# Reads of weight sums moved behind those of the second MLP's inputs, and gates and first scans moved ahead, in a one-core linear-attention and two-MLP kernel

## The chip, the cores and the metric

The kernel runs on one core of one Trainium2 chip. The metric is the device time of one execution in microseconds. Beside the timed runs there is one execution taken by the hardware profiler; all rows below are from it. Engines are named as in the profile: PE is TensorE (PEld its weight load), ACT is ScalarE, DVE is VectorE, POOL is GpSimd, SP is SyncE, which issues nearly all DMAs from one in-order queue.

## What is computed

A gated linear attention (4 batches, 8 heads, 768 positions, head size 48), then a gated MLP with an RMS norm (384 to 1536 to 384), then a second MLP with a squared ReLU (384 to 2048 to 384), all in fp32:

```
f = 1 / (1 + exp(-f_logit))
for t in range(S):
    state = f[:, :, t, :, None] * state + einsum('bhd,bhe->bhde', k[:, :, t], v[:, :, t])
    y[:, :, t] = einsum('bhd,bhde->bhe', q[:, :, t], state)
x = y as (3072, 384)
xn = x / sqrt(mean(x * x) + 1e-6) * rms_g
x = (silu(xn @ w_gate) * (xn @ w_val)) @ w_out
out = (relu(x @ w_in) ** 2) @ w_out2
```

## The kernel before

**Work and stages.** The attention is cut into 24 units: a chunk of 128 positions of one batch (six chunks, four batches). Four units fill a group of 512 tokens, and the first MLP runs over six groups. To keep fp32 accuracy every matmul of the MLPs is made three times, with operands split into a high and a low part (`fp32r`); ACT makes the high part, DVE subtracts it for the low part.

The opening `first()` follows an order written by hand: it converts the first MLP's weights, computes units 0 to 7 and runs group 0. `phase1()` runs groups 1 to 5. A group has 12 steps f; each has three *blocks* of nine 512-column matmuls on PE: G (gate projection), V (value projection) and O (output projection, of the step before). I write G5 for block G of step 5. After G, ACT computes the sigmoid product `sg`; after V, DVE multiplies it with V (L971, "the product"), ACT rounds it to `hh` (L974), and DVE makes `hl` (L976). G and V have one PSUM bank each: block G of a step needs the sigmoid of the step before to be done, block V the product of the step before. `phase2()` runs the second MLP over four sets of 768 tokens; its weight products use 15 sums of weights and inputs instead of 18 products.

**What sets the order.** Between the blocks `phase1` puts other work by *segments*: three a step, numbered through, segment s of group gi beginning at 36 gi. `plan_unit(u, s)` gives each instruction of an attention unit a segment relative to s, that of its scores: `load_gates` at -9 (DMA of both gates' logits), `gate` at -3 (two ACT passes over 128x1024: L296, L297), `scan_b` at -2 (DVE scan of the reversed gates and a reciprocal: L308, L309) with `keep_end` (ACT), `scan_a` and `mul_k` at -1 (second DVE scan, product with k: L316, L319), `mul_q` (L322) and `scores` at 0, `kv` at 6, `state_add` (DVE, L492) at 7. In a segment the planned work stands ahead of the first MLP's own sigmoid, product or rounding. Scores use two PSUM banks; one of them also holds `kv` of the unit before until `state_add` has read it. Units 8 to 23 are planned so; 8 to 11 stand closer together (scores at segments 40, 47, 54, 60) than the later ones (nine segments apart).

`plan_work` places the conversion of the second MLP's weights: loads of the raw 64-bit words, bit operations (L561, L568, L578), sums of weight blocks (`w2_sum`, L710), splits (`w2_split`: ACT L664, DVE L665) and their writes to DRAM (L667). It goes through these jobs in order and gives each the first segment at which a count of planned DVE and ACT time stays under a cap. `gate` and `scan_b` are part of that count, so moving them moves conversion jobs.

**The end of the first MLP.** In group 5 (`last0` is its first segment) the job `open` closes the pools of the raw words and the attention (`open_late`) and at once starts eight reads of weight sums, `wa` (L1031, 384 KB each), into the pool opened in their place. From segment `last0 + 9` the job `x3` reads the second MLP's inputs `x3` (L1051: three tiles, each in a piece of 512 and one of 256 columns) into slots that weights of the first MLP have left. From segment `last0 + 12` the jobs `("x", p)` split them and their sums into `xc` (ACT L1092, DVE L1093; sums L1081). The first split (p = 9) reads tile `x3_0`, the second a difference of `x3_0` and `x3_2`, the third a sum with `x3_1`. SP waits for a DMA's slot, and for the DMA eight issues earlier, before it issues; what stands behind waits too.

Of the kernel before, what the change touches and what calls it, by code (L numbers as in the profile page):

```python
# [22 lines left out]
KT = DM // P  # L23
# [166 lines left out]
def tile_linear_attention_moe(  # L190
# [29 lines left out]
    N = UG * C  # L220
    NT = 3 * C
# [449 lines left out]
    def w2_plain(key, nm, a, b):  # L671
        if nm not in w2t:
            w2t[nm] = w2_tile(nm)
        w2_split(key, w2f[key], w2t[nm][:, a], w2t[nm][:, b])
# [37 lines left out]
    def w2_part(i, c):  # L712
        t, b = w2c[i, c]
        w2_split(("c", i, c), t[:, b], t[:, 2 + b], t[:, b])

    def w2_spare(i, key):
        t, _ = w2c[i, 2]
        w2_split(key, w2f[key], t[:, 1], t[:, 3])
# [34 lines left out]
    def at(where, s, fn):  # L753
        where.setdefault(max(s, NG), []).append(fn)
# [3 lines left out]
    def plan_unit(u, s):  # L758
        starts[u] = s
        for k, fns in (  # L760
            (-9, (load_gates,)), (max(-9, starts.get(u - 2, 0) + 7 - s), (load_v,)),
            (max(-9, starts.get(u - 2, 0) + 9 - s), (load_qk,)),
            (-3, (gate,)), (-2, (scan_b, keep_end)), (-1, (scan_a, mul_k)),
            (0, (mul_q, k_turn, decay)), (1, (masked,)), (2, (k_back,)), (3, (norm, power)), (4, (x_scale,)),
            (5, (x_turn, kcopy)), (6, (x_back,)), (7, (state_add,)), (10, (x_high, x_low)),
        ):
            for fn in fns:
                if fn not in (load_gates, load_qk, load_v) or u > 2 * UG:
                    at(side, s + k, lambda fn=fn: fn(u))
                    planned.setdefault(s + k, []).append(fn.__name__)  # L770
        for k, fn in ((0, scores), (2, attend), (6, kv)):
            at(tail, s + k, lambda fn=fn: fn(u))
            room[s + k] = room.get(s + k, 0) + TAIL[fn.__name__]

    NG = 3 * F1
    for gi in range(1, NU - 1):
# [3 lines left out]
        scan_b=(1.4, 0), keep_end=(0, 0.2), scan_a=(1.2, 0), mul_k=(0.7, 0), mul_q=(0.7, 0), masked=(1.4, 0),  # L780
# [23 lines left out]
    def job(name, fn, dve=0.0, act=0.0, after=()):  # L804
        work.append((name, fn, (dve, act), after))

    def conversion(pair, after=()):
        job(("load", pair), lambda: w2_load(pair), after=after)

    def bits(pair, after=()):  # L810
        job(("scale", pair), lambda: w2_scale(pair), act=0.9, after=((("load", pair), 3),) + after)
        for n, c in enumerate((0.55, 0.96, 0.96)):
            job(("bits", pair, n), lambda n=n: w2_bits(pair, n), dve=c, after=((("scale", pair), 1),))

    def sums(i, cs, after=()):
        for n, x in enumerate(W_SUMS[cs]):
            act = x[1] == "="
            job(("sum", i, cs, n), lambda n=n: w2_sum(i, cs, n), dve=0 if act else 0.3, act=0.3 if act else 0, after=after)

    def split(name, fn, after=()):  # L820
        job(name, fn, dve=0.56, act=0.51, after=after)

    def plan_work():
        gone = ()
        for i in range(F2 // 3):
            a = tuple(("a", 3 * i + f) for f in range(3))
            b = tuple(("b", 3 * i + f) for f in range(3))
            pa, pb, pc = (a[0], a[1]), (a[2], b[0]), (b[1], b[2])
            if i == 0:
                conversion(pa)  # L830
                conversion(pb)
            bits(pa)
            bits(pb)
            sums(i, (0, 1))
            for c in (0, 1):
                split(("part", i, c), lambda i=i, c=c: w2_part(i, c), ((("sum", i, (0, 1), 5), 1),))
            sums(i, (2,))
            split(("part", i, 2), lambda i=i: w2_part(i, 2), ((("sum", i, (2,), 3), 1),))
            split(("plain", b[0]), lambda i=i, k=b[0]: w2_spare(i, k))
            sums(i, (3, 4), after=((("part", i, 1), 2),))  # L840
            conversion(pc, after=((("plain", b[0]), 2),))
            for c in (3, 4):
                split(("part", i, c), lambda i=i, c=c: w2_part(i, c), ((("sum", i, (3, 4), 5), 1),))
            bits(pc)
            if i + 1 < F2 // 3:
                na, nb = (("a", 3 * i + 3), ("a", 3 * i + 4)), (("a", 3 * i + 5), ("b", 3 * i + 3))
            else:
                na, nb = (("a", F2 - 1), ("b", F2 - 1)), None
            for n, k in enumerate(pc):
                split(("plain", k), lambda k=k, n=n, nm=f"b{3 * i + 1}": w2_plain(k, nm, 2 * n, 2 * n + 1))  # L850
                if n == 0:
                    conversion(na, after=((("bits", pc, 2), 1),))
            if nb:
                conversion(nb, after=((("plain", pc[1]), 2),))
        bits(na)
        for n, k in enumerate(na):
            split(("plain", k), lambda k=k, n=n: w2_plain(k, "last", 2 * n, 2 * n + 1))
        job(("open",), open_late, after=((("plain", na[1]), 1), (None, last0 + 2)))
        job(("x3",), lambda: (x3_tiles(), x3_load(0)), after=((None, last0 + 9),))
        freed = [2, 6, 8, 12, 14, 18, 20, 24, 26, 30, 32, 36]  # L860
        for n, p in enumerate(X_KEYS):
            f = next(f for f, c in enumerate(freed) if c >= n + 4)
            at_least = ((None, last0 + 3 * (f + 1) + 3), (("x3",), 3))
            for q in X_NEEDS.get(p, ()):
                job(("xsum", q), lambda q=q: x_sum(q, r_tile(f"xs_{q}")), dve=0.56, after=at_least)
            split(("x", p), lambda p=p: (x_tile(p), x_split(p)))
            work[-1] = work[-1][:3] + (at_least,)

        for b in range(10):
            f = next(f for f, c in enumerate(freed) if c >= b + 21)  # L870
            job(("b", b), lambda b=b: fetch_b(b), after=((None, last0 + 3 * (f + 1) + 3),))

        for name, fn, cost, after in work:
            s = max([NG, when.get("last", 0)] + [when[a] + g if a else g for a, g in after])
            while any(c and (busy(s)[e] + c > CAP + room.get(s, 0) or crowd(s, e) + c > 0) for e, c in enumerate(cost)):
                s += 1
            for e, c in enumerate(cost):
                busy(s)[e] += c
            when[name] = when["last"] = s
            at(side, s, fn)  # L880
# [7 lines left out]
    pend, nxt, parts = [], [], []  # L888
# [124 lines left out]
    def open_late():  # L1013
        upper.close()
        L["as"] = pool("late_w", bufs=8, reuse_waits="tile")
        L["r"] = pool("late_r", bufs=18, reuse_waits="tile")
        for c in range(8):
            fetch_part()

    parts_order = [(s, i, c) for s in range(NS) for i in range(NSET + 1) for c in ((0, 1, 4, 2, 3) if i < NSET else (0,))]  # L1020
    part_tiles = {}
# [2 lines left out]
    def fetch_part():  # L1024
        if fetched[0] == len(parts_order):
            return
        s, i, c = parts_order[fetched[0]]
        fetched[0] += 1
        t = L["as"].tile([P, 2, DM], F32R, tag="as", name=f"wa{s}_{i}_{c}")
        src = w2d["c", i, c] if i < NSET else w2d["a", F2 - 1]  # L1030
        nc.sync.dma_start(t.bitcast(F32), src)  # L1031
        part_tiles[s, i, c] = t
# [6 lines left out]
    def r_tile(nm):  # L1039
        return L["r"].tile([P, NT], F32, tag="r", name=nm)  # L1040

    def x3_tiles():
        L["x3"] = [wp.tile([P, 2, NT], F32, tag="w", name=f"x3_{k}") for k in range(KT)]

    def x3_load(s):
        o, g = 2 * NT * s, 0
        while g < 2 * NT:
            gi, c = divmod(o + g, N)
            n = min(N - c, 2 * NT - g)
            for k in range(KT):  # L1050
                nc.sync.dma_start(  # L1051
                    L["x3"][k].rearrange("p a t -> p (a t)")[:, g:g + n], x3d[gi][:, k, c:c + n]
                )
            g += n

    def xb(k, j):
        return L["x3"][k][:, j]
# [6 lines left out]
    def x_tile(p):  # L1064
        XT[p] = wp.tile([P, 2, NT], F32R, tag="w", name=f"xc{p}")
# [9 lines left out]
    def x_sum(p, t):  # L1075
        def arg(x):
            return xb(*x) if isinstance(x, tuple) else XS[x]

        XS[p] = t
        op, a, b = X_SUMS[p]  # L1080
        nc.vector.tensor_tensor(t, arg(a), arg(b), op=ALU.add if op == "+" else ALU.subtract)  # L1081
# [7 lines left out]
    def x_split(p, put=None):  # L1089
        src = xb(*X_PLAIN[p]) if p in X_PLAIN else XS[p]  # L1090
        t = XT[p]
        nc.scalar.copy(t[:, 0], src)  # L1092
        (put or run)(lambda: nc.vector.tensor_sub(t[:, 1], src, t[:, 0].bitcast(F32)))  # L1093
# [335 lines left out]
```

## Time and profile before

| | |
|---|---|
| median of 3 runs | 957.01 us (955.17 to 957.71) |
| profiled execution | 951.61 us |
| its span in the trace | 949.7 us |
| PE busy | 923.9 us (97%) |
| DVE, ACT busy | 644.6 us (68%), 488.5 us (51%) |
| mean granted PE clock | 0.988 of full speed |

The span is the time between the first and the last instruction of the trace; the execution's own time is 1.9 us more. A row of a wait list names who waited and for whom; a row of a timeline gives start, duration, and in brackets the idle time before it with what ended it. An idle engine costs nothing by itself: only what delays the end of PE's work does. The granted clock is given as a share of full speed: 1.00 is 2.4 GHz, 0.50 is 1.2 GHz.

### The profile page before, as it was taken

The page shows a single profiled execution, that of the slowest core. Times are in us where ns is not written, and L with a number is a line of the kernel's source. Part 1 is how long each engine was busy: PE and PEld are TensorE (multiplying, and loading weights), DVE is VectorE, ACT ScalarE, POOL GpSimd, SP SyncE. Part 2 cuts the span into 40 slices and gives each one's busy share as a digit, 9 for nine tenths or more (in the row PEclk, how much of TensorE's full clock was granted, in tenths as well). Part 3 has the DMA queues.
Part 4 walks back from the last instruction along what each step waited for, and adds up shares of the span by engine and source line. Part 5 has one row for each costly group of instructions (what it writes and reads, how often), then busy time and mean ns, then how long its engine had stood idle before and what let it go on. Part 6 is the DMA issues. An engine that isn't in the chain of part 4 may idle for free.

```text
span 949.7 us, 15747 instructions
## 1 busy us (share of the span) xinstructions
PE 923.9 (97%) x5945; PEld 813.3 (86%) x5945; DVE 644.6 (68%) x1147; ACT 488.5 (51%) x1020; POOL 31.4 (3%) x54
## 2 busy tenths in 40 slices
PE   6899999989999999999998899999999999999997
PEld 4778877878888888788887689999999999999997
DVE  7899967666777777766643635756775677666552
ACT  6876654544455544454441425556555554655451
POOL 3210000000000000000000000000000000000000
PEclk8899999999999999999999899999999999999999
DMA  9456434466457467455256056540744075406300
GB/s 340 178 190 215 154 136 121 144 203 199 124 192 219 132 207 242 146 201 172 70 180 232 1 199 240 193 151 24 232 148 151 4 240 167 125 17 190 118 26 29
DMA packets 78387, 148.48 MB, mean 156 GB/s; under 512 B 17248, under 2 KB 44000, under 8 KB 78304
## 3 DMA queue, kind: packets, MB, share of 16 engines
q1 hardware_dynamic: 78304, 147.39, 47.4%
q8 instruction: 49, 0.80, 0.4%
q14 instruction: 34, 0.28, 0.1%
HBM read 115.12 MB, written 32.24 MB: 155 GB/s over the span
## 4 chain that ended last, share of the span: by engine, by line
PE 89%; DVE 3%; DMA 2%; ACT 1%; issue 0%; SPq 0%; ACTq 0%; DVEq 0%
PE o L730 7%; PE o L728 7%; PE o L729 7%; PE X L1105 7%; PE Y L1105 6%; PE v L728 5%; PE g L728 5%; PE acc L728 5%; PE v L730 5%; PE v L729 5%; PE acc L730 5%; PE acc L729 5%; PE g L730 5%; PE g L729 5%; PE sc L341 2%; PE T L1105 2%
## 5 line engine op out<-in xcount | busy, mean ns | idle before, releaser
L730 PE MATMUL o<-wb,h 128*128 128x384 f32 x384 | 128.6, 335 | 0.0
L729 PE MATMUL o<-wb,h 128*128 128x384 f32 x384 | 128.3, 334 | 0.0
L728 PE MATMUL o<-wb,h 128*128 128x384 f32 x384 | 128.3, 334 | 0.0
L974 ACT CAST hh<-sg 128x512 fp32r<-128x512 f32 x72 | 44.7, 621 | 112.3 <-DVE sg L971 112.2
L971 DVE TENSOR_TENSOR sg<-v,sg 128x512 f32<-128x512 f32 x72 | 49.5, 688 | 54.4 <-PE v L730 52.3
L1105 PE MATMUL X<-xc,wa 128*128 128x384 f32 x360 | 82.5, 336 | 0.0
L730 PEld LDWEIGHTS o<-wb,h 128*128 128x128 f32 x384 | 72.1, 188 | 0.5
L728 PEld LDWEIGHTS o<-wb,h 128*128 128x128 f32 x384 | 72.1, 188 | 0.0
L729 PEld LDWEIGHTS o<-wb,h 128*128 128x128 f32 x384 | 72.1, 188 | 0.0
L966 ACT ACTIVATE sg<-g 128x512 f32<-128x512 f32 x72 | 42.7, 594 | 55.8 <-PE g L730 52.9
L1105 PE MATMUL Y<-xc,wa 128*128 128x384 f32 x300 | 68.3, 335 | 0.0
L1105 PEld LDWEIGHTS X<-xc,wa 128*128 128x128 f32 x360 | 63.7, 188 | 1.8 <-ACT d L1180 1.2
L1184 DVE TENSOR_TENSOR c<-T,c 128x384 f32<-128x384 f32 x40 | 22.3, 557 | 52.5 <-PE T L1105 43.4
L976 DVE TENSOR_TENSOR hl<-sg,hh 128x512 fp32r<-128x512 f32 x72 | 49.3, 685 | 7.8 <-ACT hh L974 7.8
L1105 PEld LDWEIGHTS Y<-xc,wa 128*128 128x128 f32 x300 | 53.3, 188 | 0.7 <-DVE c L1184 0.6
L1135 DVE TENSOR_TENSOR h<-d,h 128x384 fp32r<-128x384 f32 x60 | 32.8, 554 | 26.2 <-ACT h L1134 26.1
L728 PE MATMUL g<-xh,wh_o 128*128 128x512 f32 x108 | 43.8, 406 | 4.8 <-ACT sg L966 4.8
L1134 ACT CAST h<-d 128x384 fp32r<-128x384 f32 x60 | 30.2, 511 | 34.4 <-PE o L730 34.4
L1180 ACT COPY d<-X 128x384 f32<-128x384 f32 x40 | 19.1, 478 | 54.7 <-PE X L1105 54.7
L728 PE MATMUL v<-xh,wh_v 128*128 128x512 f32 x108 | 43.8, 406 | 0.2 <-DVE sg L971 0.2
L728 PE MATMUL v<-xh,wh_g 128*128 128x512 f32 x108 | 43.9, 406 | 0.0
L728 PE MATMUL g<-xh,wh_g 128*128 128x512 f32 x108 | 43.6, 404 | 0.0
(192 smaller groups left out, 2240.9 us busy)
## 6 DMA issues: line engine op xcount, KB each, us to landing
wa<-w2d_c SPq DMA_DIRECT2D x100, 384.0 KB, 3.4
raw<-in_w_dram SPq DMA_DIRECT2D x18, 768.0 KB, 4.3
ff<-in_ff_dram SPq DMA_DIRECT2D x20, 516.0 KB, 4.5
qk<-in_qk_dram SPq DMA_DIRECT2D x20, 512.0 KB, 6.2
w2d_c<-ws_c SPq DMA_DIRECT2D x50, 192.0 KB, 4.2
raw_a<-in_w_dram SPq DMA_DIRECT2D x22, 384.0 KB, 4.4
wb<-w2d_b SPq DMA_DIRECT2D x16, 384.0 KB, 3.7
v<-in_vp_dram SPq DMA_DIRECT2D x24, 192.0 KB, 4.6
```

What stands on the lines that cost most here:

```text
L728: nc.tensor.matmul(o, lh, rh, start=first, stop=False)
L729: nc.tensor.matmul(o, lh, rl, start=False, stop=False)
L730: nc.tensor.matmul(o, ll, rh, start=False, stop=last)
L966: nc.scalar.activation(dd["s", f], dd["g", f], AF.Silu)
L971: nc.vector.tensor_mul(dd["s", f], dd["v", f], dd["s", f])
L974: nc.scalar.copy(dd["h", f][0], dd["s", f])
L976: nc.vector.tensor_sub(dd["h", f][1], dd["s", f], dd["h", f][0].bitcast(F32))
L1105: nc.tensor.matmul(o, w[a], x[:, b], start=first and n == 0, stop=last and n == 2, skip_group_check=True,)
L1134: nc.scalar.copy(t[:, 0], r)
L1135: later(lambda: nc.vector.tensor_sub(t[:, 1], r, t[:, 0].bitcast(F32)))
L1180: nc.scalar.copy(t, bk[b])
L1184: nc.vector.tensor_add(t, bk[b], t)
```

## The change

Three edits. `gate` goes from segment -3 to -5 and `scan_b` with `keep_end` from -2 to -3. The eight first reads of weight sums leave `open_late` and become a job `parts`, two segments or more after the job `x3`. And `x3_load` reads tile by tile, in the order 0, 2, 1, both pieces of a tile together, where it had read the first pieces of all tiles and then the second ones.

```diff
@@ plan_unit
-            (-3, (gate,)), (-2, (scan_b, keep_end)), (-1, (scan_a, mul_k)),
+            (-5, (gate,)), (-3, (scan_b, keep_end)), (-1, (scan_a, mul_k)),
@@ plan_work
         job(("x3",), lambda: (x3_tiles(), x3_load(0)), after=((None, last0 + 9),))
+        job(("parts",), lambda: [fetch_part() for _ in range(8)], after=((("x3",), 2),))
@@ open_late
         L["r"] = pool("late_r", bufs=18, reuse_waits="tile")
-        for c in range(8):
-            fetch_part()
@@ x3_load
-        o, g = 2 * NT * s, 0
-        while g < 2 * NT:
-            gi, c = divmod(o + g, N)
-            n = min(N - c, 2 * NT - g)
-            for k in range(KT):
+        for k in (0, 2, 1):
+            o, g = 2 * NT * s, 0
+            while g < 2 * NT:
+                gi, c = divmod(o + g, N)
+                n = min(N - c, 2 * NT - g)
                 nc.sync.dma_start(
                     L["x3"][k].rearrange("p a t -> p (a t)")[:, g:g + n], x3d[gi][:, k, c:c + n]
                 )
-            g += n
+                g += n
```

On SP, in group 5, behind the last write of a plain weight (`w2d_b_15`), the kernel before has the reads `wa` (of eight alike, the first and the last stand here) and then those of `x3`:

```order
L667 DMA w2d_b_15_5256<-ws_last_5250 128x384 x2
L1031 DMA wa0_0_0_5281<-w2d_c_0_0_1884 128x768
...
L1031 DMA wa0_1_4_5295<-w2d_c_1_4_3092 128x768
L1051 DMA x3_0_5321<-x3d_0_81 128x512
L1051 DMA x3_1_5322<-x3d_0_81 128x512
L1051 DMA x3_2_5323<-x3d_0_81 128x512
L1051 DMA x3_0_5321<-x3d_1_82 128x256
```

The same place of the changed kernel:

```order
L667 DMA w2d_b_15_5256<-ws_last_5250 128x384 x2
L1050 DMA x3_0_5305<-x3d_0_81 128x512
L1050 DMA x3_0_5305<-x3d_1_82 128x256
L1050 DMA x3_2_5307<-x3d_0_81 128x512
L1050 DMA x3_2_5307<-x3d_1_82 128x256
L1050 DMA x3_1_5306<-x3d_0_81 128x512
L1050 DMA x3_1_5306<-x3d_1_82 128x256
L1030 DMA wa0_0_0_5339<-w2d_c_0_0_1886 128x768
```

The six reads of `x3` now stand directly behind the writes and ahead of all eight `wa`, and the first two fill tile 0.

On ACT, at the beginning of group 1 (`x3o` is the copy of group 0's result, `ff8` the gates of unit 8, `sg_1_0` and `hh_1_0` the sigmoid and the rounding of step 0), before:

```order
L909 COPY x3o_0_2_1517<-acc_0_2_719 128x512
L966 ACTIVATE sg_1_0_1537<-g_1_0_1521 128x512
L296 ACTIVATE ff8_1430<-ff8_1430 128x8x128
L297 ACTIVATE ff8_1430<-ff8_1430,half_92 128x8x128
L974 CAST hh_1_0_1552<-sg_1_0_1537 128x512
L312 COPY ends_94<-ff8_1430 128x4
```

and now:

```order
L910 COPY x3o_0_2_1517<-acc_0_2_719 128x512
L296 ACTIVATE ff8_1430<-ff8_1430 128x8x128
L297 ACTIVATE ff8_1430<-ff8_1430,half_92 128x8x128
L967 ACTIVATE sg_1_0_1539<-g_1_0_1521 128x512
L312 COPY ends_94<-ff8_1430 128x4
L975 CAST hh_1_0_1555<-sg_1_0_1539 128x512
```

Unit 8's gate has moved ahead of the sigmoid (it can't go further, since segment 36 is the first), and the copy of the ends ahead of the rounding. From unit 10 on the gate stands between a sigmoid and its rounding.

On DVE, in step 7 of group 1, between the first scan of unit 11 and the state addition of unit 10 (`ws_c0_2`, `ws_c0_3` hold weight sums, `qk11` k and q of unit 11), before:

```order
L308 SCALAR_TENSOR_TENSOR ff11_1904<-ff11_1904,floor_89 128x516
L309 RECIPROCAL seed_90<-ff11_1904 128x4
L971 TENSOR_TENSOR sg_1_7_2079<-v_1_7_2081,sg_1_7_2079 128x512
...
L665 TENSOR_TENSOR ws_c0_2_1983<-ws_c0_2_1983 128x384
L665 TENSOR_TENSOR ws_c0_2_1983<-m_a2_1647,ws_c0_2_1983 128x384
L710 TENSOR_TENSOR ws_c0_3_2152<-m_a2_1647 128x128
L710 TENSOR_TENSOR ws_c0_3_2152<-ws_c0_3_2152,m_a2_1647 128x128
L710 TENSOR_TENSOR ws_c0_3_2152<-m_a0_1577,ws_c0_3_2152 128x128
L492 TENSOR_TENSOR state2_99<-kv10_2158,state2_99 48x4x48 x2
```

and now:

```order
L308 SCALAR_TENSOR_TENSOR ff11_1907<-ff11_1907,floor_89 128x516
L309 RECIPROCAL seed_90<-ff11_1907 128x4
L404 SCALAR_TENSOR_TENSOR xg10_2094<-y10_2036,rs10_2075,gB_96 128x384
L665 TENSOR_TENSOR ws_c0_2_1931<-ws_c0_2_1931 128x384
L972 TENSOR_TENSOR sg_1_7_2082<-v_1_7_2084,sg_1_7_2082 128x512
...
L665 TENSOR_TENSOR ws_c0_2_1931<-m_a2_1710,ws_c0_2_1931 128x384
L710 TENSOR_TENSOR ws_c0_3_2152<-m_a2_1710 128x128
L710 TENSOR_TENSOR ws_c0_3_2152<-ws_c0_3_2152,m_a2_1710 128x128
L710 TENSOR_TENSOR ws_c0_3_2152<-m_a0_1577,ws_c0_3_2152 128x128 x2
L710 TENSOR_TENSOR ws_c0_3_2152<-m_a0_1577 128x128
L492 TENSOR_TENSOR state2_99<-kv10_2161,state2_99 48x4x48 x2
```

Between the product of step 7 and the state addition there is one split subtraction (L665) less and there are two sums (L710) more; the scan stands ahead of the product in both. PE's instructions and their order are the same in both kernels.

## Rows read from the trace of the kernel before

**Rows 1.** The page: busy time, share of the span and instructions of each engine.

```profile
PE 923.9 (97%) x5945; PEld 813.3 (86%) x5945; DVE 644.6 (68%) x1147; ACT 488.5 (51%) x1020; POOL 31.4 (3%) x54
```

**Rows 2.** PE's waits, whole span: waiter and releaser, us in total, times, longest.

```profile
PE g L728 <- ACT sg L966: 4.8, 1, 4.8
...
PE sc L341 <- DVE state L492: 2.6, 1, 2.6
...
PE sc L341 <- DVE qk L322: 1.2, 1, 1.2
```

**Rows 3.** Timeline of PE, group 5: start, us, engine, line, operation, [idle before].

```profile
513.53 0.39 PE L728 MATMUL g<-xh,wh_g 128*128 128x512 f32 x1
...
519.43 0.39 PE L730 MATMUL acc<-hh,wl_v 128*128 128x512 f32 x1
524.57 0.79 PE L728 MATMUL g<-xh,wh_o 128*128 128x512 f32 x1 [4.76 <-ACT sg L966]
...
542.28 0.50 PE L728 MATMUL v<-xh,wh_v 128*128 128x512 f32 x1 [0.23 <-DVE sg L971]
```

**Rows 4.** Stretches: us; busy us of PE, PEld, DVE, ACT, POOL; PEclk; DMA; GB/s.

```profile
195.00:200.00 5.00, 2.91 (x22) 2.52 (x23) 3.15 (x8) 0.00 (x0) 0.00 (x0) 1.00 0.92 246
...
525.00:526.00 1.00, 1.00 (x3) 0.73 (x3) 0.64 (x2) 0.29 (x1) 0.00 (x0) 0.50 0.00 0
```

**Rows 5.** Timeline of ACT, group 5, steps 3 and 4.

```profile
512.49 0.62 ACT L974 CAST hh<-sg 128x512 fp32r<-128x512 f32 x1 [2.18 <-DVE sg L971]
521.91 0.51 ACT L1092 CAST xc<-x 128x384 fp32r<-128x384 f32 x1 [8.80 <-DMA x<-x3d]
...
523.93 0.59 ACT L966 ACTIVATE sg<-g 128x512 f32<-128x512 f32 x1
```

**Rows 6.** Timeline of SP's DMA issues, group 5: start, us of all in the row.

```profile
505.13 0.89 SPq L667 DMA_DIRECT2D w2d_b<-ws_last  x2
507.79 5.13 SPq L1031 DMA_DIRECT2D wa<-w2d_c  x8
513.02 4.79 SPq L1051 DMA_DIRECT2D x<-x3d  x6
```

**Rows 7.** DMA issues of the whole span: count, KB each, median us to landing.

```profile
ff<-in_ff_dram SPq DMA_DIRECT2D x20, 516.0 KB, 4.5
...
x3d<-x3o SPq DMA_DIRECT2D x18, 256.0 KB, 2.3
...
x<-x3d SPq DMA_DIRECT2D x12, 256.0 KB, 4.8
```

**Rows 8.** Timelines of ACT and DVE, group 1, unit 8.

```profile
130.61 1.96 ACT L909 COPY x3o<-acc 128x512 f32<-128x512 f32 x3 [2.01 <-PE acc L730]
...
134.57 1.05 ACT L296 ACTIVATE ff<-ff 128x1024 f32<-128x1024 f32 x1
...
136.85 0.62 ACT L974 CAST hh<-sg 128x512 fp32r<-128x512 f32 x1
...
138.21 0.67 DVE L976 TENSOR_TENSOR hl<-sg,hh 128x512 fp32r<-128x512 f32 x1
...
140.51 0.68 DVE L322 TENSOR_TENSOR qk<-qk,ff 128x512 f32<-128x512 f32 x1
```

**Rows 9.** Timeline of DVE, group 1, ahead of unit 11's scores.

```profile
189.74 0.68 DVE L971 TENSOR_TENSOR sg<-v,sg 128x512 f32<-128x512 f32 x1
...
194.91 0.55 DVE L665 TENSOR_TENSOR ws_c<-m_a,ws_c 128x384 fp32r<-128x384 f32 x1
195.38 0.28 DVE L710 TENSOR_TENSOR ws_c<-m_a 128x128 f32<-128x128 f32 x1
...
196.23 0.72 DVE L492 TENSOR_TENSOR state<-kv,state 48x192 f32<-48x192 f32 x2
```

**Rows 10.** Timelines of SP and ACT, group 2, gates of unit 14.

```profile
242.80 0.43 SPq L284 DMA_DIRECT2D ff<-in_ff_dram  x1
...
251.26 0.60 ACT L966 ACTIVATE sg<-g 128x512 f32<-128x512 f32 x1 [1.29 <-PE g L730]
...
254.09 0.62 ACT L974 CAST hh<-sg 128x512 fp32r<-128x512 f32 x1 [2.23 <-DVE sg L971]
```

## Prediction

> **What bounds the kernel now.** First the busy line of the page: TensorE is busy for 97% of the span and VectorE, the next engine, for 68% (PEld is TensorE's own weight load) [rows 1]. So time can only be won where TensorE waits or runs slowly, and I read TensorE's waits next. After the opening part (the first 50 us, which the change leaves alone) only three are above 0.3 us: 4.8 us for a sigmoid of the first MLP, 2.6 us and 1.2 us for operands of the attention scores [rows 2]. The rest of the trace is matmul behind matmul.
>
> The long wait is the one to follow. In TensorE's timeline [rows 3] G4 begins at 513.53 and the last matmul of O3 at 519.43; that is three blocks (G4, V4, O3) of nine matmuls in 6.13 us, 2.04 us a block. G5 should begin at 519.66 and begins at 524.57, 4.91 us late, with matmuls of 0.79 us where 0.39 stood before. The granted clock says why: 1.2 GHz (0.50) in the slice at 525 us, after TensorE had done nothing for those microseconds; through the 2.6 us wait at 195 us it had stayed at 2.4 GHz (1.00) [rows 4].
>
> Who was late? ScalarE ends hh of step 3 at 512.49 + 0.62 = 513.11 and then stands before the first X split (xc), which waits 8.80 us for the read of x3. The sigmoid of step 4, whose input was ready at 515.6, stands behind that split in ScalarE's order and runs at 523.93 [rows 5]; G5 needs its PSUM bank. And x3 was late because SP had issued eight weight reads (wa, 384 KB each) ahead of it: SP is through with the last writes at 505.13 + 0.89 = 506.02, waits 1.8 us more for them to land before the first wa, spends 5.13 us on the eight, and starts on x3 only at 513.02 [rows 6].
>
> **The change, part by part.** (1) **x3 ahead of wa.** The order of SP shows the six x3 reads right behind the last ws_last write, wa after them. The x3 tiles lie in slots of first-MLP weights, and do not wait for the raw pool to close, as wa does. The slots wait for TensorE at most up to O1, which is over by 507.4 (three blocks before G4's 513.53); I take 506.02, and 507.4 as the late end. Six issues at the 0.4 us that SP's writes take there (0.89 for two) are 2.5 us: 506.0 to 508.6, or 507.4 to 509.9. A 256 KB transfer on this queue lands 2.3 us after its issue (write of x3 to DRAM); the x3 reads themselves, in company, take 4.8 [rows 7]. The first split needs only x3_0, now read first in both pieces: by 506.9 + 2.3 = 509.2, at the worst ends 508.2 + 4.8 = 513.0. The last piece is there by 509.9 + 4.8 = 514.7, and x3_1 is first used in the third split, three to four us behind the first. ScalarE comes to the first split at 513.11. So it does not wait: the 8.80 us go whole.
>
> What is late next? The splits are a chain that goes to and fro between ScalarE and VectorE, and the first MLP's own steps stand in it. Its tightest point is the product of step 6: TensorE's V7 needs it, waited 0.23 us for it and began at 542.28 [rows 3], 20.37 us behind the first split at 521.91. Begun at 513.11 the chain reaches it at 533.48. An undisturbed TensorE is at V7 seven blocks after 519.66 (G5, V5, O4, G6, V6, O5, G7): 519.66 + 14.30 = 533.96. The chain is 0.48 us ahead, so V7 starts at 533.96 and not at 542.28: **8.3 us**, of which 4.9 are the wait and 3.4 the slow clock and the small wait at V7. Bounds: every microsecond that the reads land after 513.6 is given back; I put 7.3 to 8.4.
>
> The eight wa reads move from 507.8 to about 508.6: eight issues in 5.1 us as before. Their first reader comes after O10 of this group, seven steps of three blocks or 43 us behind 519.66, so this costs nothing; if that cover were gone it would be the 6 us of six x3 reads at most. The wb reads behind them on SP wait for TensorE anyway. Later x3 reads change only their order among themselves and are made many products before use: nothing.
>
> (2) **Gates at -5, first scans at -3.** No instruction is added; gate (two passes on ScalarE), first scan, reciprocal and the copy of the ends move for units 8 to 23, and the planner shifts conversion work around them. TensorE waits at two of these sixteen scores only.
>
> Unit 8 (1.2 us): the gate began at 134.57, behind the sigmoid of step 0; ScalarE had been free since 130.61 + 1.96 = 132.57, and the gate now stands ahead of that sigmoid. It starts 2.0 us earlier, the scan runs before the step's product instead of behind it, and the next subtraction (hl) follows hh, which ended at 136.85 + 0.62 = 137.47, and not the scan at 138.21: 0.74 us earlier. Everything from there to the product with q (140.51 + 0.68 = 141.19) is unbroken VectorE work (hl, second scan, product with k, product with q) [rows 8]. The wait shrinks by 0.7.
>
> Unit 11 (2.6 us): here the second half of the scores wants a PSUM bank that the state addition of unit 10 must free first. VectorE works without a break from the product at 189.74 over eleven more instructions to that addition at 196.23 [rows 9]. The scan lies ahead of this stretch, before and now. Within it the planner takes out one split subtraction (0.55) and puts in two sums (0.28 each): 0.01 longer. The wait stays. Its bounds are +0.6 (both sums count, the subtraction does not leave) and -0.2.
>
> Here a rule speaks against the change. What the row shows is a full clock through this wait [rows 4]. The Trainium skill (TensorE: Matmul & The Clock Gate, section "Part 1: The HAM clock gate") says that an idle array falls to half rate and is released by activity; the trace agrees at 525 us, and shows no fall at 195. By that rule, with a longer wait here, the sum would lose again what (1) wins on the clock; by the row it keeps it. That is the third rival.
>
> Units 9 and 10 get up to 0.8 us of conversion work put ahead of their second scan, while TensorE reached their scores without a wait. I allow 0.2 us for both, between 0 and 0.8.
>
> Units 12 to 23 had no waits. What the early gate could add is a hold-up of ScalarE: it now stands between the sigmoid of a step and its hh. Typical (unit 14): the gates' inputs are issued at 242.80 and land 4.5 us later [rows 7], 247.3; the sigmoid of the step runs at 251.26 to 251.86 and hh ran at 254.09 [rows 10]. The gate takes at most 2.3 us (unit 8's ran from 134.57 to before hh at 136.85 [rows 8]), from 251.9 to 254.2. The inputs are 4.6 us early, and hh is held up by 0.1 us, which nobody waits for. Part (2) is 0.7 - 0.2 = **0.5 us**, between -0.7 and +0.9.
>
> **Sum.** 8.3 + 0.5 = 8.8 us. The profiled execution took 951.61 us, so 942.8. It lies 5.4 us under the median of the runs shown, 957.01, for which the profile gives no reason; I take the same distance for the changed kernel: **948.2 us**.
>
> **Rivals.** *First, the split chain takes the place of the read.* Its lead at V7 is only 0.48 us. For it: VectorE and ScalarE wait for each other at each split. Against it: against a TensorE that had itself lost 8 us the same chain cost only the 0.23 us at V7, and nothing at the steps behind it. If the reads come 3 us later than I think, V7 waits 2.5 us: 950.7.
> *Second, the change does not do what it says:* SP's x3 reads wait for something else until about 513 (a slot, a queue). Against it: all nearby PE releases lie before 507.4. Then only (2) is left: 956.5.
> *Third, unit 11's wait grows to that of step 5.* VectorE has no free time there. Were it as long as G5's and followed by the same slow clock, it would cost 4.8 - 2.6 = 2.2 us more and 3.4 for the clock: 948.2 + 5.6 = 953.8.
> *Fourth, slower:* the gate waits for its input on ScalarE, with hh and the next sigmoid behind it. It decides when inputs land more than 4.6 us later than now, and TensorE then waits only when hl comes after the next V, about 4 us on. To end above 959.9 it must lose 8.8 + 2.9 = 11.7 us over 16 units, 0.7 us each beyond that. Nothing in the trace points that way.
>
> **How the numbers follow.** Forecast 0.78, first rival 0.10, second 0.05, third 0.05, fourth 0.02. A measurement of this kernel tells about 0.3% from no change (954.1 to 959.9). Forecast, first and third rival are faster: 0.93; second the same: 0.05; slower 0.02. For the range: the runs shown lie 3.6 to 6.1 us above the profiled one, which alone gives 946.4 to 948.9; with the bounds of (2) and a little of the first rival 945.2 to 951.4.
>
> **What would show it.** Right: in the wait list the row of the sigmoid (4.8) is gone, the x3 reads are issued by 507.5, G5 follows O3 at once, the granted clock is 1.00 from 500 to 560 us; the unit 8 wait is 0.3 to 0.5, the unit 11 wait 2.4 to 2.8. Wrong: a new row of TensorE waiting for VectorE's product (first rival), x3 reads at 513 (second), a granted clock of 0.50 near 200 us (third), ScalarE's gate waiting for a DMA (fourth).

## The result, and the profile after

| | before | after |
|---|---|---|
| median of four runs each | 956.19 us (955.17 to 957.71) | 948.24 us (947.26 to 949.40) |
| profiled execution | 951.61 us | 947.26 us |
| its span | 949.7 us | 945.4 us |

The ratio of after to before is 0.9916, with an interval of 0.9896 to 0.9936: 8.0 us faster (956.19 x 0.0084). The forecast time, 948.2, was met. That it was met so closely is luck: the traces show that the second term of the sum was wrong, and the base it started from was too high by about as much.

**The reads.** SP's issues and ACT in group 5 of after (start, duration, engine, line, operation), to be held against [rows 5, 6]:

```profile
509.10 0.89 SPq L667 DMA_DIRECT2D w2d_b<-ws_last  x2
510.09 2.81 SPq L1050 DMA_DIRECT2D x<-x3d  x6
512.99 4.68 SPq L1030 DMA_DIRECT2D wa<-w2d_c  x8
```

```profile
516.46 0.62 ACT L975 CAST hh<-sg 128x512 fp32r<-128x512 f32 x1 [2.18 <-DVE sg L972]
516.99 0.51 ACT L1091 CAST xc<-x 128x384 fp32r<-128x384 f32 x1
...
519.81 0.60 ACT L967 ACTIVATE sg<-g 128x512 f32<-128x512 f32 x1 [0.51 <-PE g L730]
```

The six x3 reads follow the last write at once, with no wait for a slot, and wa comes behind them. G4 is 3.98 us later in this trace than in that of before; counted from it, the first read goes out at 506.1, as forecast. The two pieces of `x3_0` land at 513.07 and 513.38, 3.6 us ahead of the first split, which has no bracket: the 8.80 us are gone. PE's blocks G4, G5 and V7, the product that V7 needs, and PE's stretch at 525 us, to be held against [rows 3, 4]:

```profile
517.51 0.39 PE L728 MATMUL g<-xh,wh_g 128*128 128x512 f32 x1
...
523.63 0.39 PE L728 MATMUL g<-xh,wh_o 128*128 128x512 f32 x1
...
537.91 0.39 PE L728 MATMUL v<-xh,wh_v 128*128 128x512 f32 x1
```

```profile
536.83 0.68 DVE L972 TENSOR_TENSOR sg<-v,sg 128x512 f32<-128x512 f32 x1
```

```profile
525.00:530.00 5.00, 5.00 (x24) 4.14 (x23) 3.26 (x7) 2.04 (x4) 0.00 (x0) 1.00 0.00 2
```

G4 to G5 is 6.12 us, three undisturbed blocks; G4 to V7 is 20.40 us where it was 542.28 - 513.53 = 28.75. That is 8.35 us gained, and the granted clock is 1.00 from 500 to 560 us. The product ends at 537.51, 0.40 us ahead of V7.

**The gates.** PE's waits behind the opening (80 to 945 us) in after, against [rows 2]:

```profile
PE sc L341 <- DVE state L492: 2.5, 1, 2.5
PE sc L341 <- issue: 1.3, 1, 1.3
PE sc L341 <- DVE qk L322: 0.6, 1, 0.6
PE sc L341 <- PE g L730: 0.5, 2, 0.2
```

The sigmoid's row (4.8) is gone. Unit 8 waits 0.57 instead of 1.15 (row "qk"), unit 11 2.47 instead of 2.60 (row "state"). But there are three waits that before did not have: 0.2 us each at the scores of units 15 and 18, and 1.33 at those of unit 21. They are put down to "issue" and to PE's own G block; what really came late is the product with q, whose end the scores follow within 0.1 us in all three (units 15 and 18: 288.74 to 288.84 and 356.11 to 356.22). For unit 21 it stands on DVE at the start of group 4, in after and then in before:

```profile
415.78 0.56 DVE L665 TENSOR_TENSOR ws_c<-m_a,ws_c 128x384 fp32r<-128x384 f32 x1 [2.07 <-ACT ws_c L664]
416.26 0.28 DVE L710 TENSOR_TENSOR ws_c<-m_a 128x128 f32<-128x128 f32 x1
416.46 0.69 DVE L977 TENSOR_TENSOR hl<-sg,hh 128x512 fp32r<-128x512 f32 x1
417.06 1.23 DVE L308 TENSOR_TENSOR_SCAN ff<-ff,floor 128x516 f32<-128x516 f32 x1
...
420.24 0.68 DVE L972 TENSOR_TENSOR sg<-v,sg 128x512 f32<-128x512 f32 x1
...
423.16 0.69 DVE L322 TENSOR_TENSOR qk<-qk,ff 128x512 f32<-128x512 f32 x1
```

```profile
416.32 0.67 DVE L971 TENSOR_TENSOR sg<-v,sg 128x512 f32<-128x512 f32 x1
...
419.23 0.68 DVE L322 TENSOR_TENSOR qk<-qk,ff 128x512 f32<-128x512 f32 x1
```

In after a split subtraction of the second MLP's weights (L665) has come to stand ahead of everything. It waits 2.07 us for its rounding on ACT, which is behind three output copies there, and hl, the scan, five sums or splits and the product queue behind it. From the product to the product with q it is 2.91 to 2.92 us in both kernels; so the lateness is there already at the product. The product with q ends at 423.85, and the scores start at 423.95.

**The two traces, added up** (start of the product of a step, and of V7, before minus after): the opening to the first product of group 1, 136.13 - 139.00 = -2.87; to step 3 of that group +0.68 (unit 8); to its step 9 +0.11 (unit 11); to step 3 of group 5 -1.90 (units 15, 18, 21); G4 to V7 +8.35. The sum is 4.37, and V7 is 4.37 earlier. The change made 8.35 - 1.1 = 7.2 us of it; the opening, whose code is the same, was 2.87 us longer in this execution.

### The profile page after: what moved, and what is told of

It reads as the page before. It is cut to its first block, busy times and chain, and to the rows that moved or that the text cites. A ratio compares the mean times of both kernels' runs of the same rounds, so it can differ in the third digit from the quotient of the medians.

```text
span 945.4 us, 15739 instructions
## 1 busy us (share of the span) xinstructions
PE 921.7 (97%) x5945; PEld 810.1 (86%) x5945; DVE 644.3 (68%) x1147; ACT 487.9 (52%) x1020; POOL 31.1 (3%) x54
## 4 chain that ended last, share of the span: by engine, by line
PE 91%; DMA 3%; DVE 2%; ACT 2%; issue 1%; SPq 0%; POOL 0%; DVEq 0%; POOLq 0%; ACTq 0%
PE o L730 7%; PE o L728 7%; PE o L729 7%; PE X L1104 7%; PE Y L1104 6%; PE v L728 5%; PE g L728 5%; PE acc L728 5%; PE acc L729 5%; PE acc L730 5%; PE v L730 5%; PE v L729 5%; PE g L730 5%; PE g L729 5%; PE T L1104 2%; PE R L1104 2%
```

## Experiments

The theory that the two traces suggest, A in the expectations: the reads win all of the time, since the splits were what V7 waited for, and the gates lose about 1 us, since conversion work is shifted in front of products with q. Its rivals: B, the gates gain 0.5 us as forecast; C, the early gate itself does the harm; the others are named where they are tried.

**The kernel before, once more.** Was the opening of 136.13 us what this kernel always does?

> The kernel before, once more, for what a second profiled execution of it shows. Ratio 1.000. If the opening's length differs from one execution to the next, the product of the first step of group 1 (136.1 us in the first trace, 139.0 us in that of the changed kernel, whose opening is the same code) lies elsewhere by a microsecond or more; if 136.1 us is what this kernel always does, it is there within 0.3 us, and the 2.9 us are something the change does to the opening. All waits of TensorE behind the opening should be as in the first trace, within 0.2 us: 1.15, 2.5 and 4.8 us.

The ratio is 1.0008 (0.9992 to 1.0025); the profiled execution took 956.52 us. The first product of group 1:

```profile
138.08 0.69 DVE L971 TENSOR_TENSOR sg<-v,sg 128x512 f32<-128x512 f32 x1 [5.68 <-PE v L730]
```

It is 1.95 us later than in the first trace of the same program. Over all thirteen traces of this study this product lies at 136.1 to 136.6 six times and at 138.0 to 140.0 seven times, whatever the kernel. The two traces of before part at ten filler matmuls of the opening (`du`), first trace, then second:

```profile
31.04 2.33 PE L738 MATMUL du<-mask 128*128 128x512 bf16 x10
```

```profile
31.83 3.62 PE L738 MATMUL du<-mask 128*128 128x512 bf16 x10
```

They end 2.08 us later in the second. From 32 to 34 us the granted clock is 1.00 in the first and 0.50 in the second. It is so in all thirteen: 1.00 there and 2.33 us for the fillers in the six with the short opening, 0.50 or 0.51 and 2.96 to 4.00 us in the seven with the long one.

And there is a second difference. The stretches behind unit 11's wait, in this trace and then in that of after (the number before the DMA share and GB/s is the granted clock):

```profile
199.00:201.00 2.00, 1.93 (x14) 1.78 (x14) 0.25 (x1) 0.00 (x0) 0.00 (x0) 0.50 0.74 207
201.00:203.00 2.00, 2.00 (x6) 1.57 (x6) 1.04 (x2) 0.00 (x0) 0.00 (x0) 0.50 1.05 393
```

```profile
199.00:201.00 2.00, 1.83 (x17) 1.64 (x18) 0.88 (x3) 0.00 (x0) 0.00 (x0) 1.00 0.85 214
201.00:203.00 2.00, 2.00 (x10) 1.65 (x9) 0.77 (x2) 0.00 (x0) 0.00 (x0) 1.00 1.04 366
```

After the same wait (2.59 us here, 2.60 in the first trace of before, 2.47 in after) PE runs at 1.2 GHz here and at 2.4 GHz there. From the product of step 6 of group 1 to that of step 9 it takes 29.91 us here, 27.05 in the first trace: 2.86 us lost. Together that is 1.95 + 2.86 = 4.8 us of the 4.9 between the two profiled executions of this kernel (956.52 and 951.61). Two smaller differences nearly cancel: the first split waits 8.35 us here and not 8.80, which gives 0.45 back, and behind V7 0.66 are lost again. For the same reason the sigmoid's wait was not the 4.8 that I expected but 4.3, with 0.7 more at G6. The first one's distance to the median, for which I had found no reason, is about as long as these two clock differences together.

**The two parts apart.** The first part alone is the changed kernel with one line as before; the second part alone is the kernel before with that line changed.

```diff
-            (-5, (gate,)), (-3, (scan_b, keep_end)), (-1, (scan_a, mul_k)),
+            (-3, (gate,)), (-2, (scan_b, keep_end)), (-1, (scan_a, mul_k)),
```

> Only the first part of the change: the reads of the second MLP's inputs tile by tile and ahead of those of weight sums; gates and first scans stand as before. Theory A (from the two traces: the reads give all of the gain, and the moved gates and scans lose 0.8 us gained at units 8 and 11 and 1.9 us more at units 15, 18 and 21): 8.3 us under the kernel before, ratio 0.9913, that is about 1 us under the changed kernel; TensorE's wait for the scores of unit 8 is 1.1 to 1.2 us as before, of unit 11 2.5 to 2.6, at units 15, 18 and 21 under 0.2. Rival B (the gates and scans gain 0.5 us, as I had predicted; the waits at units 15, 18 and 21 are chance or come from the reads): 7.5 us under the kernel before (0.9922), 0.5 us over the changed kernel, with waits at units 15, 18 and 21 here too.

> Only the second part of the change: gate at -5, first scan at -3, with the planner's shift; the reads stand as before. Theory A: 1 us slower than the kernel before (ratio 1.001); the wait for the scores of unit 8 falls to 0.5 to 0.6 us, and there are waits of 0.2 to 0.3 us at units 15 and 18 and of 1.3 us at unit 21; the wait for the sigmoid of step 4 in group 5 stays at 4.8 us, with the slow clock behind it. Rival B: 0.5 us faster (0.9995), no waits at units 15, 18 and 21. The two lie within a measurement by their times, so the waits decide.

The reads alone give 0.9915 (0.9894 to 0.9935), the gates alone 1.0013 (0.9998 to 1.0028). PE's waits behind the opening (80 to 945 us), reads alone, then gates alone:

```profile
PE sc L341 <- DVE state L492: 2.6, 1, 2.6
PE sc L341 <- DVE qk L322: 1.1, 1, 1.1
```

```profile
PE g L728 <- ACT sg L966: 4.8, 1, 4.8
PE sc L341 <- DVE state L492: 2.5, 1, 2.5
PE sc L341 <- issue: 1.3, 1, 1.3
PE sc L341 <- DVE qk L322: 0.6, 1, 0.6
PE sc L341 <- PE g L730: 0.5, 2, 0.2
PE v L728 <- DVE sg L971: 0.2, 1, 0.2
```

Theory A holds row by row. The whole gain is the first part's, and the three new waits come with the second. By time alone the second part can't be told from no change; its loss of about 1 us is read from the waits.

**Is it the earlier gate, or the work that the planner shifts?** Two kernels, one for each half of the second part: the changed kernel with the planner's count as before (first diff), and the first part alone with the planner's count of the changed kernel (second).

```diff
-                    planned.setdefault(s + k, []).append(fn.__name__)
+                    kp = {"gate": -3, "scan_b": -2, "keep_end": -2}.get(fn.__name__, k)
+                    planned.setdefault(s + kp, []).append(fn.__name__)
```

```diff
-                    planned.setdefault(s + k, []).append(fn.__name__)
+                    kp = {"gate": -5, "scan_b": -3, "keep_end": -3}.get(fn.__name__, k)
+                    planned.setdefault(s + kp, []).append(fn.__name__)
```

> The changed kernel, but the planner counts gates and first scans where they stood before, so that no conversion work is shifted; the instructions themselves stand as in the changed kernel. If the loss at units 15, 18 and 21 comes from the shifted conversion work (theory A): no waits there above 0.2 us, the unit 8 wait at 0.5 to 0.6 us, some 9 us under the kernel before (0.9906). If it comes from the gates and scans standing earlier by themselves (rival C): waits as in the changed kernel, 1.3 us at unit 21, and the same time as that kernel (0.9916).

> The first part of the change, gates and first scans where they stood before, but the planner counts them where the changed kernel has them, so that the conversion work is shifted as there and nothing else of the second part is done. Theory A (the shifted conversion work alone makes the waits at units 15, 18 and 21): 0.2 to 0.3 us at units 15 and 18 and 1.3 us at unit 21, unit 8 at 1.1 to 1.2 us as before, some 1.9 us over the first part alone, ratio 0.9935. Rival I (it takes both, the shifted work and the earlier gates): none of the three waits above 0.2 us, ratio 0.9915.

With the gates moved and the conversion work left in place the ratio is 0.9913 (0.9891 to 0.9935) and PE's list is short:

```profile
PE sc L341 <- DVE state L492: 2.5, 1, 2.5
PE sc L341 <- DVE qk L322: 0.6, 1, 0.6
```

The time can't be told from that of the changed kernel (0.9916); the waits decide, and against rival C. So the early gate by itself does here what I had forecast for it: unit 8 wins, units 12 to 23 have no waits. The reverse came out far from both theories, at 1.0031 (1.0014 to 1.0047):

```profile
PE sc L341 <- PE g L730: 5.1, 8, 0.9
PE sc L341 <- issue: 3.0, 2, 1.6
PE sc L341 <- DVE state L492: 2.8, 1, 2.8
PE sc L341 <- DVE qk L322: 1.2, 1, 1.2
PE sc L341 <- PE kv L476: 0.9, 1, 0.9
```

That is 13.0 us of waits where the reads alone have 3.7. The planner takes the segment of the first scan for free and fills it with sums and splits while the scan still stands there; DVE then comes late to the product with q of ten units (9 and 13 to 21, rows "PE g" and "issue"). My 1.9 us were wrong as a price of the shift: they are what is left of it once the scan has gone too. The shift and the move are thus not two small effects side by side but a loss of some 9 us in waits (11 by the ratios, whose intervals are wide) and a return of most of it, and the changed kernel keeps the rest of the loss at units 15, 18 and 21.

**The reads, in half the dose and without the tile order.** The first is the first part alone with the lines below; the second is the first part alone with `x3_load` as in the kernel before.

```diff
         L["r"] = pool("late_r", bufs=18, reuse_waits="tile")
+        for c in range(4):
+            fetch_part()
...
-        job(("parts",), lambda: [fetch_part() for _ in range(8)], after=((("x3",), 2),))
+        job(("parts",), lambda: [fetch_part() for _ in range(4)], after=((("x3",), 2),))
```

> The first part of the change in half its dose: four of the eight weight-sum reads stay ahead of the reads of the second MLP's inputs, four go behind; tile order as in the changed kernel, gates and scans as before. Four reads take 2.6 us on SP and wait 1.8 us before the first, so the first split should wait some 3 to 5 us on ScalarE, where it waited 8.8 and now none. Theory A (the chain of splits has a lead of 0.4 us at V7 of group 5, and all lateness beyond that is TensorE's): 2.6 to 4.6 us lost against the first part alone, seen as waits of TensorE for products or sigmoids up to V7; ratio to the kernel before 0.994 to 0.996. Rival D (only the sigmoid of step 4 counts, which had 8.8 - 4.9 = 3.9 us of room): at most 1 us lost, ratio 0.9915 to 0.9925, no wait at V7.

> The first part of the change without its tile order: the six input reads go ahead of the weight sums, but piece by piece over the tiles as in the kernel before. The first split then needs the first and the fourth read instead of the first two, about 1 us later on SP (0.47 us a read). Theory A: they still land before ScalarE comes to the first split, at most 0.5 us after it, so ratio 0.9915 as for the first part alone, with a wait of 0 to 0.4 us at V7. Rival E (the tile order carries part of the gain): 1 to 3 us lost against the first part alone (0.9925 to 0.9945), the first split waiting 1 us or more for its read.

With four wa reads ahead the ratio is 0.9951 (0.9935 to 0.9967), 3.4 us over the reads alone. The first split and V7:

```profile
518.54 0.51 ACT L1093 CAST xc<-x 128x384 fp32r<-128x384 f32 x1 [3.64 <-DMA x<-x3d]
```

```profile
515.33 0.39 PE L728 MATMUL g<-xh,wh_g 128*128 128x512 f32 x1
...
521.45 0.39 PE L728 MATMUL g<-xh,wh_o 128*128 128x512 f32 x1
...
538.92 0.50 PE L728 MATMUL v<-xh,wh_v 128*128 128x512 f32 x1 [0.18 <-DVE sg L972]
```

G5 (521.45) is not late at all, so the sigmoid of step 4 had room, as rival D says; V7 comes 23.59 us behind G4 instead of 20.40, and 3.19 of the 3.64 us are lost all the same, from V5 to V7 (1.63 of them between O4 and G6). That is theory A: beyond a lead of about half a microsecond each microsecond of lateness at the first split is PE's. Five traces with waits there of 3.64 to 9.55 us (this one, both of before, the gates alone and the next experiment) have one rule: G4 to V7 takes 20.40 us plus that wait less 0.45.

The tile order does nothing here: 0.9921 (0.9895 to 0.9947), the first split without a wait, and no wait of PE in group 5. The reads that the first split needs, the first and the fourth, land by 517.20, and it starts at 518.27: the lead is large enough for either order.

**Was the slow clock a price of its own?** The kernel before, with PE kept at work through its long wait.

```diff
+                if gi == NU - 1 and f == 5:
+                    dense(22, ps.tile([P, 2, 2 * C], F32, tag="pa", name="fill"))
                 step_piece("G", gi, f)
```

> The kernel before, with 22 more bf16 matmuls of 512 columns (about 4.7 us of work whose result nobody reads) on TensorE ahead of G5 of group 5, so that it does not stand idle while it waits for the sigmoid of step 4. The question is whether the 3.4 us behind that wait belong to the slow clock or to the late splits. Theory A: the chain of splits needs 20.4 us from the first split to the product that V7 wants, at whatever clock TensorE runs; the clock stays at 1.00, TensorE comes to V7 3.4 us earlier and waits there (or at the blocks ahead of it) for those 3.4 us; ratio 1.000. Rival F (the clock alone was the price): no wait up to V7, 3.4 us faster, ratio 0.9964.

The ratio is 1.0020 (1.0003 to 1.0037). The filler, G5, G6 and V7:

```profile
522.89 4.92 PE L738 MATMUL fill<-mask 128*128 128x512 bf16 x22
528.56 0.50 PE L728 MATMUL g<-xh,wh_o 128*128 128x512 f32 x1 [0.74 <-ACT sg L966]
...
537.30 0.50 PE L728 MATMUL g<-xh,wh_g 128*128 128x512 f32 x1 [1.01 <-ACT sg L966]
...
546.27 0.50 PE L728 MATMUL v<-xh,wh_v 128*128 128x512 f32 x1 [0.23 <-DVE sg L971]
```

Behind the filler the matmuls run at full speed (0.39 to 0.50 us, not 0.79), and PE spends the time so won on waits at V5, O4 and G6: G5 to V7 takes 17.71 us here, as in the first trace of before with its slow clock, and as in the second, where the clock was back at 1.00 some 4 us behind G5. V7 stands 20.38 us behind the first split (525.89), as it does at 1.2 GHz: 20.37 in the first trace of before and in the gates alone, 20.38 in the second trace of before and in half the dose. Where the splits are on time, V7 stands 20.91 to 20.92 behind the first (after and six more kernels). So the splits set V7 in the kernel before, and the slow clock lay in their shadow. Theory A is right; the kernel is 0.2% (1.9 us) slower rather than equal. The reads, 0.75 us later in this trace (9.55 against 8.80), are a part of that; the rest is not explained.

**A version without the wait of unit 11.** Its scores, one segment later, stand behind the state addition that frees their bank. The line below was put into the kernel with all gates early and the planner's count as before, and into the first part alone with gate and first scan early for unit 8 only.

```diff
-            plan_unit((gi + 1) * UG + j, gi * NG + ((4, 11, 18, 24) if gi == 1 else (-3, 6, 15, 24))[j])
+            plan_unit((gi + 1) * UG + j, gi * NG + ((4, 11, 18, 25) if gi == 1 else (-3, 6, 15, 24))[j])
```

> The changed kernel with the planner's count of gates and scans as before, and the scores of unit 11 one segment later (61 instead of 60), behind the state addition of unit 10 that frees their PSUM bank. Theory G: the wait of 2.5 us at unit 11 goes, and with it the stretch of 1.2 GHz clock behind it that four of six profiled executions show (5.5 us long, 2.4 to 2.8 us lost); no other wait of TensorE over 0.6 us behind the opening; 4 to 5 us under the kernel with the wait (947.1), so 942 to 943, ratio 0.986 to 0.987. Rival H (VectorE's work without a break moves the wait on, to the scores of unit 11 or 12 themselves): a wait of 1 us or more at unit 11 or 12, gain under 1.5 us, ratio 0.990 or more.

> The first part of the change, gate and first scan early for unit 8 alone, the planner's count as before, and the scores of unit 11 in segment 61. In the run with all gates early a wait of 0.93 us for kv of unit 12 stood at the start of group 2, where ScalarE ran the early gate of unit 13 ahead of the key copy. Theory A: that wait is gone, TensorE waits 0.5 to 0.6 us at unit 8 and nowhere else above 0.3 us behind the opening, 0.9 us under the run with all gates early (0.9878 there), ratio 0.987. Rival J (the key copy is late for another reason, the three output copies ahead of it): the wait of 0.9 us stays.

> The kernel with the planner's count as before, all gates early and the scores of unit 11 in segment 61, once more beside the run with the early gate of unit 8 alone. Ratio 0.987 to 0.989, the 0.93 us wait for kv of unit 12 there again, the clock at 1.00 from 190 to 210 us.

All gates early give 0.9878 (0.9847 to 0.9908) and, the second time, 0.9887 (0.9867 to 0.9906); unit 8 alone gives 0.9870 (0.9853 to 0.9887). PE's waits (80 to 945 us) with all gates early (the second time), then with unit 8 alone:

```profile
PE kv L476 <- ACT ktok L436: 0.9, 1, 0.9
PE sc L341 <- DVE qk L322: 0.6, 1, 0.6
```

```profile
PE sc L341 <- DVE qk L322: 0.6, 1, 0.6
```

The wait of 2.5 us is gone, and in all three traces the clock stays at 1.00 from 190 to 210 us. From the product of step 6 of group 1 to that of step 9 they take 24.2 to 24.3 us, where the traces with the wait take 26.9 or more. The first run's 942.4 us is within theory G's 942 to 943, but its ratio is not (the kernel before had 954.2 in that comparison), and theory G had no room for the new wait: with all gates early both traces have one of 0.93 us for the key copy. With unit 8 alone, without the early gate of unit 13, it is not there (theory A; the output copies of rival J stand as before). The gate works there by way of DVE, in the first run with all gates early:

```profile
228.79 0.56 DVE L665 TENSOR_TENSOR ws_b<-m_b,ws_b 128x384 fp32r<-128x384 f32 x1 [2.17 <-ACT ws_b L664]
```

The gate (226.12 to 228.36 on ACT) holds up the rounding of a split; its subtraction, this row, stands ahead of the product, and so hh, the output copies and the key copy come late. Which of the two kernels is faster the times do not tell. The one with unit 8 alone, 942.8 us against 955.77 us of before in the same comparison, is better than the changed kernel too: its interval ends at 0.9887, that of the changed kernel begins at 0.9896.

## Why the prediction was right, and where it was not

**The first term (8.3 us) was right** and for its reasons: no slot held the reads up (issued behind the last write, six in 2.81 us where I had 2.5), the first split did not wait, and the chain of splits was ahead of V7 by 0.40 us where I had 0.48. The trace shows 8.35. What was wrong is how I divided it, 4.9 us for the wait and 3.4 for the slow clock: with the clock kept up the 3.4 us were lost as waits. The number held because I had taken it from the split chain to V7, not from the two prices.

**The second term (+0.5 us) was wrong:** about -1.1 in the traces (0.68 + 0.11 - 1.90), below its bound of -0.7. Unit 8 won what I forecast (0.68 for 0.7, though its wait only fell to 0.57, just outside the 0.3 to 0.5 that I had named), unit 11 stayed (2.47, within 2.4 to 2.8), units 9 and 10 did not wait, so my 0.2 was not needed. The step that failed is that on units 12 to 23, which I put at nothing: it cost 1.90 us, at units 15, 18 and 21. I asked there what the early gate holds up on ACT, which in after is nothing that PE waits for, and not what the planner puts on DVE into the place that gate and scan leave. I had counted shifted work for units 9 to 11, and should have done it for each unit up to the product with q.

**The distance to the median (5.4 us) was no property of the kernel.** The profiled execution of before had the short opening, and it kept the clock behind unit 11; that of after had the long opening, and lay 1.0 us under its median. For the profiled execution itself the sum gave 942.8, and it took 947.26. The forecast fell on 948.2 since a gain put too high (8.8, where the measured medians give 8.0 and the traces 7.2) stood against a base put too high (957.01, now 956.19). That the two agree to 0.1 us is luck.

**The rivals.** The first and second did not come, though half the dose shows the first's mechanism at work: lateness beyond the lead goes to V7. Of the fourth one sign came, without its price: the gate of unit 9 waits for its input on ACT, for 0.21 us, and no wait of PE follows:

```profile
146.33 1.06 ACT L296 ACTIVATE ff<-ff 128x1024 f32<-128x1024 f32 x1 [0.21 <-DMA ff<-in_ff_dram]
```

No other gate behind the opening waits so. Of the third, the wait of unit 11 did not grow, but its clock did what that rival says in eight of the ten traces with this wait, the second of the kernel before among them. The rule of the Trainium skill that I weighed there (TensorE: Matmul & The Clock Gate, section "Part 1: The HAM clock gate") is that an idle array falls to half rate. Those eight traces agree with it; the one that I had, the first of before, and that of after stay at 1.00.

## What to carry to other kernels

When a step of a planned schedule moves, look at what the planner puts where it was: the engine's queue up to the next operand that TensorE needs is the place to count, unit by unit. When a stall and a slow clock stand together, ask which chain sets the next common point before adding their prices; a wait that is filled with other matmuls keeps the clock and may win nothing. And before one profiled execution serves as a base, see whether its distance to the median has a place in the trace.

## What the runs showed that was not expected

The granted clock behind one and the same wait is not the same from execution to execution. Ten traces have a wait of 2.5 to 2.8 us at unit 11's scores. In two the clock stays at 1.00; in eight it falls to 0.50 or 0.51 for some microseconds. From the product of step 6 of group 1 to that of step 9 the seven of them with no other new wait there take 28.6 to 30.1 us, against 26.9 and 27.05 in the two: 1.6 to 3.1 us. In the three without the wait it stays at 1.00. What decides it in the ten stays open. The opening's length, 136.1 to 140.0 us in the same code, is in good part the same thing: the clock at the fillers from 32 to 34 us, 1.00 in the six short openings and 0.50 or 0.51 in the seven long ones. Why it differs there stays open too; nothing was tried on it.
